# Sliding-window attention gated by a GLU: q weights ahead of x tile 3, four more products of zeros, and reciprocals and one tile's transposes moved from the DMA queue to the matrix engine

## The chip, the cores and the metric

The kernel runs on one core of a Trainium2 chip. A core has a matrix engine (PE, TensorE; its weight loads are listed as PEld), a vector engine (DVE), a scalar engine (ACT), a general engine (POOL), and a queue engine (SP) that issues all of this kernel's DMAs. The engines run side by side, each through its own instructions in order, and wait for each other by semaphores. The metric is the device time in microseconds (us).

## The reference

The inputs are bf16: x (2048 x 512), wqkv (512 x 1536), wo (512 x 512), the GLU's w_gate and w_up (512 x 1792) and w_down (1792 x 512).

```python
xn  = layernorm(x)
# attention: 32 heads of 16, each position looks at 8 keys, 2 apart, behind it
qkv = xn @ wqkv
logits[s, w] = q[s] . k[s - 2*w] * 16**-0.5          # -1e9 where s - 2*w < 0
attn = softmax(logits over w)
o[s] = sum_w attn[s, w] * v[s - 2*w]
s   = o @ wo
# GLU, on the same xn
g   = silu((gelu(xn @ w_gate) * (xn @ w_up)) @ w_down)
out = x + s * g
```

Attention and GLU share the layer-normed xn; the residual is x itself.

## The kernel before

The 2048 rows are 16 tiles of 128 rows, in four chunks j of 512 rows. Each chunk goes through three stages: `glu` (14 columns of 128 features: eight 512-column products into g_ps and u_ps, Gelu and a copy on ACT, their product h on DVE), `qkv` (12 groups of four products; of the *next* chunk) and `down` (four tiles; the down products over h, silu on ACT, the product with wo, the gate and the residual on DVE, the store). Everything else (layer norm, transposes, logits, softmax, the weighted sums over v) is hung between these steps by a table, `side`: `at((stage, j, i), function, ...)` puts a function ahead of step i of a stage, in the order of the calls, and `run` issues it there. The order of every engine's instructions is that of the program text; nothing is reordered.

**Transposes.** The products need xn transposed (xnT). `transpose` (L204) does it on PE, four 128-column products with the identity into one accumulator tile, then a copy to SBUF on ACT or DVE (L217, L219). `transpose_by_dma` (L229) does it with four transposing DMAs on SP's queue. Chunk 0, and tiles 4 to 6 of chunk 1, go by PE; tile 7, the last of chunk 1, and chunks 2 and 3 go by DMA.

**Softmax division.** `denominators` (L313) sums the exponentials on PE, and DVE takes the reciprocals (L328), 128 x 128 values rs. They must be spread over four row groups and 512 columns (rb) before `divide` (L379) multiplies them into the weighted sums o_ps on DVE. `spread_reciprocals` (L331) spreads them by four 128-column products on PE (sp_ps) and a copy on ACT (L339); the last chunk does it so. `spread_by_dma` (L342) stores rs to DRAM (L344) and loads it back four times (L347); chunks 0 to 2 do it so. Chunk 0's division stands ahead of the 11th qkv group of chunk 1, those of chunks 1 and 2 ahead of the 7th qkv group of the next chunk, that of chunk 3 ahead of its last GLU column.

**Accumulators.** The tiles of the pool `mm` (g_ps, u_ps, qkv_ps, y_ps, s_ps, tr, den_ps, sp_ps, warm_ps) are four buffers in turn: a new one waits until what was in its buffer four tiles earlier has been read.

**The head.** SP requests x tiles 0 to 3 one by one (L95), then wqkv in three parts (q, k, v; L97), then the rest of x and the GLU weights. PE meanwhile multiplies zeros (`warm_up`, L221; 17 products of 256 columns, later twice four of 128). DVE takes the moments of a tile (L177), ACT the square root (L179), DVE normalizes (L199), PE transposes. The q products of the first two tiles (q_ps) follow, then tiles 2 and 3:

Of the kernel before, what the change touches and what calls it, by code (L numbers as in the profile page):

```python
# [10 lines left out]
BF16 = mybir.dt.bfloat16  # L11
F32 = mybir.dt.float32

P = 128
H = 32
# [3 lines left out]
WL = 4  # L19
WH = 2  # L20
PAD = 16
TQ = 512
# [6 lines left out]
def kernel(  # L29
# [13 lines left out]
    nc = tc.nc  # L43
    B, S, D = A_x.shape
    DF = B_w_gate.shape[1]
    NT, NC, NF, NJ = S // P, D // P, DF // P, S // TQ
    TPQ = TQ // P
# [5 lines left out]
    def pool(name, bufs, **kw):  # L53
        return ctx.enter_context(tc.tile_pool(name=name, bufs=bufs, **kw))
# [10 lines left out]
    op = pool("op", 1)  # L65
# [3 lines left out]
    dram = pool("dram", 1, space=bass.MemoryType.DRAM)  # L69
# [5 lines left out]
    wqkv_sb = wts.tile([P, NC, 3 * D], BF16, name="wqkv_sb")  # L75
# [2 lines left out]
    wd_sb = wts.tile([P, NF, D], BF16, name="wd_sb")  # L78
    wo_sb = wts.tile([P, NC, D], BF16, name="wo_sb")
    vT = dram.tile([D, SV], BF16, name="vT")  # L80
    rs_d = [dram.tile([P, P], BF16, name=f"rs_d{j}") for j in range(NJ - 1)]

    def load_x(t, n=1):
        nc.sync.dma_start(
            out=x_sb[:, t : t + n, :],
            in_=x2d[t * P : (t + n) * P, :].rearrange("(t p) d -> p t d", p=P),
        )

    def load_w(dst, src, lo, hi):
        nc.sync.dma_start(  # L90
            out=dst[:, :, lo:hi], in_=src.rearrange("(k p) n -> p k n", p=P)[:, :, lo:hi]
        )

    for t in range(TPQ):
        load_x(t)  # L95
    for i in range(3):
        load_w(wqkv_sb, A_wqkv, i * D, (i + 1) * D)  # L97
    load_x(TPQ, TPQ)
    for i, (lo, hi) in enumerate(((0, DF // 2), (DF // 2, DF))):
# [4 lines left out]
    def load_late_weights():  # L104
        nc.sync.dma_start(out=wd_sb[:], in_=B_w_down.rearrange("(k p) n -> p k n", p=P))
        for g in range(NC):
            nc.sync.dma_start(
                out=wo_sb[:, g, :],
                in_=bass.AP(
                    tensor=A_wo.tensor, offset=g * 4 * D, ap=[[D, 4], [DH * D, H], [1, D]]  # L110
                ),
            )
# [7 lines left out]
        out=vT.rearrange("(k p) n -> p k n", p=P)[:, :, 0:PAD],  # L120
        in_=warm[:, 0 : NC * PAD].rearrange("p (k n) -> p k n", k=NC),
# [54 lines left out]
    def first_moments(t):  # L176
        nc.vector.bn_stats(out=stats[:, t, :], in_=x_sb[:, t, :])  # L177
        nc.vector.bn_aggr(out=mv[:, t, :], in_=stats[:, t, :])
        nc.scalar.activation(  # L179
            out=std[:, t, :], in_=mv[:, t, 1:2], func=AF.Sqrt, bias=epsc[:], scale=1.0  # L180
        )
# [39 lines left out]
    def warm_up(n, cols):  # L221

        ps = mm.tile([P, TQ], F32, name="warm_ps", tag="mm")
        for _ in range(n):
            nc.tensor.matmul(
                ps[:, 0:cols], lhsT=warm[:, 0:P], rhs=warm[:, 0:cols], start=True, stop=True
            )
# [22 lines left out]
    st = [dict(pk={}, pv={}) for _ in range(NJ)]  # L250

    def qkv(j, fo, i0=0, n=TQ, ps=None):
        which, c = divmod(fo, NC)
        if fo == 0 and i0 == 0:
            st[j]["q"] = qp.tile([P, NC, TQ], BF16, name="q_sb")
        if ps is None:
            ps = mm.tile([P, n], F32, name="qkv_ps", tag="mm")[:]
            project(ps, wqkv_sb, fo * P, j, i0, n)
        if which == 0:
            nc.scalar.activation(out=st[j]["q"][:, c, i0 : i0 + n], in_=ps, func=AF.Copy)  # L260
        elif which == 1:
            lo = PAD + j * TQ + i0
            nc.scalar.activation(out=k_sb[:, c, lo : lo + n], in_=ps, func=AF.Copy)  # L263
        else:
            vst = sm4.tile([P, TQ], BF16, name="vst")
            nc.scalar.activation(out=vst[:], in_=ps, func=AF.Copy)  # L266
            lo = PAD + j * TQ
            nc.sync.dma_start(out=vT[c * P : (c + 1) * P, lo : lo + TQ], in_=vst[:])

    def load_v(j, wls=range(WL)):  # L270

        if wls[0] == 0:
            st[j]["va"] = vap.tile([P, DH, VW], BF16, name="v_arr")
        va = st[j]["va"]
        for wl in wls:
            nc.sync.dma_start(
                out=va[H * wl : H * (wl + 1), :, :],
                in_=bass.AP(
                    tensor=vT.tensor,
                    offset=PAD + j * TQ - WL * DIL - DIL * wl,  # L280
                    ap=[[SV * DH, H], [SV, DH], [1, VW]],
                ),
            )
# [55 lines left out]
        nc.scalar.activation(out=rb[:], in_=sp[:], func=AF.Copy)  # L339
        st[j]["rb"] = rb  # L340

    def spread_by_dma(j):  # L342

        nc.sync.dma_start(out=rs_d[j][:, :], in_=st[j]["rs"][:])  # L344
        rb = op.tile([P, TQ], BF16, name="rbd")
        for i in range(WL):
            nc.sync.dma_start(  # L347
                out=rb[H * i : H * (i + 1), :].rearrange("h (q i) -> h q i", q=4),
                in_=rs_d[j].rearrange("(q h) i -> h q i", h=H),
            )  # L350
        st[j]["rb"] = rb

    def av_product(j, g, wh):
        pv = prod.tile([P, 4, TQ], BF16, name="pv", tag="prod")
        lo = WL * DIL * (1 - wh)
        nc.vector.tensor_tensor(  # L356
            out=pv[:],
            in0=st[j]["E"][:, wh, :].unsqueeze(1).to_broadcast([P, 4, TQ]),
            in1=st[j]["va"][:, 4 * g : 4 * g + 4, lo : lo + TQ],
            op=ALU.mult,  # L360
        )
        st[j]["pv"][g, wh] = pv
# [73 lines left out]
    def at(key, fn, *args):  # L436
        side.setdefault(key, []).append((fn, args))
# [5 lines left out]
    for i in range(TPQ):  # L443
        at(("qkv", 0, i), normalize, TPQ + i)
        at(("glu", 0, 7 + i), moments, 2 * TPQ + i)
        if i < TPQ - 1:
            at(("glu", 0, i), transpose, TPQ + i)
        at(("glu", 0, 8 + i), normalize, 2 * TPQ + i)
        at(("glu", 1, 0), transpose_by_dma, 2 * TPQ + i)
        at(("glu", 1, 10 + i), moments, 3 * TPQ + i)  # L450
        at(("qkv", 2, 2 * i), normalize, 3 * TPQ + i)
        at(("glu", 2, 0), transpose_by_dma, 3 * TPQ + i)
# [4 lines left out]
    for i in range(8):  # L457
        at(("glu", 0, 12 + i) if i < 2 else ("qkv", 1, (0, 1, 3, 4, 5, 6)[i - 2]),
           av_product, 0, i // 2, i % 2)
    at(("qkv", 1, 3), denominators, 0)  # L460
    at(("qkv", 1, 3), spread_by_dma, 0)
    at(("qkv", 1, 10), av_sums, 0)
    at(("qkv", 1, 10), divide, 0)

    for j in range(1, NJ):
        for w in range(W):
            early = j > 1 and w < 3
            at(("qkv", j, 9 + w) if early else ("down", j - 1, w // 3), qk_product, j, w)
        for i in range(TPQ):
            at(("down", j - 1, i), load_v, j, [i])  # L470
        at(("glu", j, 0), logits, j)
        for i in range(8):
            at(("glu", j, 2 + i), av_product, j, i // 2, i % 2)
        at(("glu", j, 11), denominators, j)
        at(("glu", j, 11), av_sums, j)
        if j + 1 < NJ:
            at(("glu", j, 11), spread_by_dma, j)
            at(("qkv", j + 1, 6), divide, j)
        else:
            at(("glu", j, 12), spread_reciprocals, j)  # L480
            at(("glu", j, 13), divide, j)


    HT = TPQ // 2
    HQ = HT * P
    warm_up(17, TQ // 2)
    first_moments(0)
    first_moments(1)
    first_normalize(0)
# [27 lines left out]
    for i in range(NC):  # L517
        run("qkv", 0, i)
        run("qkv", 0, NC + i)
        qkv(0, 2 * NC + i)  # L520
    at(("glu", 0, 0), transpose_by_dma, 2 * TPQ - 1)
    at(("glu", 0, 0), load_v, 0)
    at(("glu", 0, 0), load_late_weights)
    for j in range(NJ):
        for fc in range(NF):
            run("glu", j, fc)
# [36 lines left out]
```

## Time and profile before

| | us |
|---|---|
| median of three runs (230.1 to 230.49) | 230.17 |
| the profiled execution | 230.49 |
| its span, first to last instruction | 228.8 |
| PE busy | 222.7 (97% of the span) |
| DVE busy | 147.6 (65%) |
| ACT busy | 130.6 (57%) |
| POOL busy | 21.7 (10%) |

Busy time is the time in which an engine has an instruction of its own at work. In a row of a timeline the first number is the start after the beginning of the span, the second how long the row's instructions took from the first start to the last end, and `x4` how many they are; in brackets, where it is there, how long the engine stood idle before them and who ended that. Products on PE are pipelined: the next starts before the last has ended, so what a group costs PE is read from its start to the next group's start. `SPq` rows are DMA requests, not transfers. A few per cent of the products' records are missing from a trace, so that a group may show three products where it has four.

### The profile page before, as it was taken

How to read it: one execution, taken by the hardware profiler on the slowest of the kernel's cores; microseconds unless marked ns; L12 is line 12 of the kernel's file. 1: busy time of each engine (PE TensorE's matmuls, PEld its weight loads, DVE VectorE, ACT ScalarE, POOL GpSimd, SP SyncE). 2: the span in 40 equal slices, each digit the busy share in tenths (PEclk: the TensorE clock that was granted, in tenths of full speed). 3: DMA queues.
4: the chain of work that ended last, by engine and by line, in shares of the span. 5: the costliest groups of instructions: out<-in, count | busy, mean ns of one | idle time of the engine just before them, and what ended most of it. 6: DMA issues, size and time to landing. Idle time of an engine off the chain costs nothing.

```text
span 228.8 us, 3516 instructions
## 1 busy us (share of the span) xinstructions
PE 222.7 (97%) x1303; PEld 106.8 (47%) x1323; DVE 147.6 (65%) x234; ACT 130.6 (57%) x215; POOL 21.7 (10%) x61
## 2 busy tenths in 40 slices
PE   7999999999999999999999999999999999999994
PEld 5865444444444444444444444444444444444453
DVE  4593996894898198865678169735449429845232
ACT  3679779764514867476721687646741387647211
POOL 1048944100000000110000000000000000000000
PEclk9999999999999999999999999999999999999999
DMA  6999599922366611110266711110038910000001
GB/s 157 357 375 376 140 175 199 315 98 80 91 153 152 135 23 29 27 29 0 92 162 152 162 29 23 26 34 6 30 104 193 202 30 3 0 0 4 23 23 46
DMA packets 29857, 24.33 MB, mean 106 GB/s; under 512 B 9488, under 2 KB 29840, under 8 KB 29840
## 3 DMA queue, kind: packets, MB, share of 16 engines
q1 hardware_dynamic: 29840, 24.11, 41.0%
q8 instruction: 10, 0.16, 0.3%
q14 instruction: 7, 0.06, 0.1%
HBM read 18.61 MB, written 4.31 MB: 100 GB/s over the span
## 4 chain that ended last, share of the span: by engine, by line
PE 94%; ACT 2%; DVE 1%; DMA 1%; issue 1%; ACTq 0%; DVEq 0%
PE y_ps L411 21%; PE u_ps L242 21%; PE g_ps L242 20%; PE qkv_ps L242 17%; PE s_ps L421 6%; PE L_ps L299 3%; PE o_ps L370 3%; DMA x_sb<-in_A_x_dram 1%; PE q_ps L242 1%; PE tr L208 1%; DVE stats L177 1%; ACT L395 1%; ACT u L397 1%; PE den_ps L319 0%; ACT xnT L217 0%
## 5 line engine op out<-in xcount | busy, mean ns | idle before, releaser
L242 PE MATMUL u_ps<-xnT,wu_sb 128*128 128x512 bf16 x223 | 57.3, 379 | 0.2
L242 PE MATMUL g_ps<-xnT,wg_sb 128*128 128x512 bf16 x214 | 56.5, 379 | 0.6 <-issue 0.2
L411 PE MATMUL y_ps<-wd_sb,h 128*128 128x512 bf16 (+1 forms) x234 | 50.9, 366 | 0.2
L399 DVE TENSOR_TENSOR h<-ge,u 128x512 bf16<-128x512 bf16 x56 | 23.8, 424 | 37.5 <-ACT u L397 36.8
L288 DVE TENSOR_TENSOR pk<-q_sb,k_sb 128x2048 bf16<-128x2048 bf16 x32 | 37.8, 1221 | 7.0 <-ACT k_sb L263 7.0
L395 ACT ACTIVATE ge<-g_ps 128x512 bf16<-128x512 f32 x56 | 33.6, 600 | 14.7 <-PE g_ps L242 14.0
L397 ACT ACTIVATE u<-u_ps 128x512 bf16<-128x512 f32 x56 | 33.6, 599 | 14.6 <-PE u_ps L242 14.4
L242 PE MATMUL qkv_ps<-xnT,wqkv_sb 128*128 128x512 bf16 (+1 forms) x203 | 40.5, 354 | 0.2
L356 DVE TENSOR_TENSOR pv<-E,v_arr 128x2048 bf16<-128x2048 bf16 x32 | 38.6, 1217 | 0.0
L411 PEld LDWEIGHTS <-h 128*128 128x128 bf16 x238 | 23.3, 98 | 25.3
L418 ACT ACTIVATE sl<-y_ps 128x512 bf16<-128x512 f32 (+1 forms) x17 | 9.7, 573 | 44.0 <-PE y_ps L411 44.0
L242 PEld LDWEIGHTS <-wu_sb 128*128 128x128 bf16 x224 | 21.9, 98 | 26.6 <-issue 0.3
L242 PEld LDWEIGHTS <-wg_sb 128*128 128x128 bf16 x224 | 21.2, 98 | 26.8 <-issue 3.0
L242 PEld LDWEIGHTS <-wqkv_sb 128*128 128x128 bf16 x224 | 21.7, 98 | 19.6 <-issue 0.4
L429 DVE TENSOR_TENSOR m<-s_ps,sl 128x512 bf16<-128x512 f32 (+1 forms) x17 | 11.2, 658 | 22.4 <-PE s_ps L421 22.4
L421 PE MATMUL s_ps<-wo_sb,oT 128*128 128x512 bf16 (+1 forms) x68 | 16.6, 366 | 0.0
L193 POOL TENSOR_TENSOR rstd<-rstd,mhalf 128x1 f32<-128x1 f32 x12 | 7.7, 638 | 78.9 <-DVE rstd L190 76.7
L266 ACT ACTIVATE vst<-qkv_ps 128x512 bf16<-128x512 f32 x16 | 9.6, 598 | 6.4 <-PE qkv_ps L242 6.4
L263 ACT ACTIVATE k_sb<-qkv_ps 128x512 bf16<-128x512 f32 (+1 forms) x20 | 10.2, 517 | 3.4 <-PE qkv_ps L242 3.2
L260 ACT ACTIVATE q_sb<-qkv_ps 128x512 bf16<-128x512 f32 (+1 forms) x16 | 8.7, 545 | 3.5 <-PE qkv_ps L242 3.3
L421 PEld LDWEIGHTS <-oT 128*128 128x128 bf16 x68 | 6.6, 98 | 7.2
L382 DVE TENSOR_TENSOR oT<-o_ps,rbd 128x1024 bf16<-128x1024 f32 x6 | 7.1, 1219 | 3.7 <-PE qkv_ps L242 3.7
(52 smaller groups left out, 119.3 us busy)
## 6 DMA issues: line engine op xcount, KB each, us to landing
v_arr<-vT SPq DMA_DIRECT2D x16, 520.0 KB, 5.1
vT<-vst SPq DMA_DIRECT2D x16, 128.0 KB, 2.8
out_dram<-o_t SPq DMA_DIRECT2D x15, 128.0 KB, 2.3
wg_sb<-in_B_w_gate_dram SPq DMA_DIRECT2D x2, 896.0 KB, 10.8
wu_sb<-in_B_w_up_dram SPq DMA_DIRECT2D x2, 896.0 KB, 10.9
wd_sb<-in_B_w_down_dram SPq DMA_DIRECT2D x1, 1792.0 KB, 16.9
wqkv_sb<-in_A_wqkv_dram SPq DMA_DIRECT2D x3, 512.0 KB
x_sb<-in_A_x_dram SPq DMA_DIRECT2D x3, 512.0 KB, 11.6
```

What stands on the lines that cost most here:

```text
L242: nc.tensor.matmul(ps, lhsT=w[:, dk, lo : lo + P], rhs=xnT[j][:, dk, i0 : i0 + n], start=(dk == 0), stop=(dk == NC - 1),)
L263: nc.scalar.activation(out=k_sb[:, c, lo : lo + n], in_=ps, func=AF.Copy)
L266: nc.scalar.activation(out=vst[:], in_=ps, func=AF.Copy)
L288: nc.vector.tensor_tensor(out=pk[:], in0=st[j]["q"][:], in1=k_sb[:, :, off : off + TQ], op=ALU.mult)
L356: nc.vector.tensor_tensor(out=pv[:], in0=st[j]["E"][:, wh, :].unsqueeze(1).to_broadcast([P, 4, TQ]), in1=st[j]["va"][:, 4 * g : 4 * g + 4, ...
L395: nc.scalar.activation(out=ge[:], in_=g_ps[:], func=AF.Gelu_apprx_tanh)
L397: nc.scalar.activation(out=u[:], in_=u_ps[:], func=AF.Copy)
L399: nc.vector.tensor_tensor(out=h[:], in0=ge[:], in1=u[:], op=ALU.mult)
L411: nc.tensor.matmul(y[:], lhsT=st[j][fc][:, tt * P : (tt + 1) * P], rhs=wd_sb[:, fc, cols], start=(fc == 0), stop=(fc == NF - 1),)
L418: nc.scalar.activation(out=sl[:, cols], in_=y[:], func=AF.Silu)
L421: nc.tensor.matmul(s[:], lhsT=st[j]["oT"][:, g, tt * P : (tt + 1) * P], rhs=wo_sb[:, g, cols], start=(g == 0), stop=(g == NC - 1),)
L429: nc.vector.tensor_tensor(out=m[:], in0=s[:], in1=sl[:, cols], op=ALU.mult)
```

## The change

The q part of wqkv is requested ahead of x tile 3. Four products of zeros of 128 columns are added behind the seventeen at the beginning. Tile 7 is transposed on PE, ahead of the fourth GLU column of chunk 0, not by DMA. In chunks 0 to 2 the reciprocals are spread by PE and ACT; chunk 0's spread stands ahead of the ninth qkv group of chunk 1 and its division where it was; in chunks 1 and 2 spread and division stand ahead of the 13th and 14th GLU column, as in chunk 3. The loads of chunk 0's v and of the late weights are issued ahead of the first GLU column without the table; the DMA transposes that stood ahead of them are gone.

```diff
-    rs_d = [dram.tile([P, P], BF16, name=f"rs_d{j}") for j in range(NJ - 1)]
...
-    for t in range(TPQ):
+    for t in range(TPQ - 1):
         load_x(t)
-    for i in range(3):
+    load_w(wqkv_sb, A_wqkv, 0, D)
+    load_x(TPQ - 1)
+    for i in range(1, 3):
         load_w(wqkv_sb, A_wqkv, i * D, (i + 1) * D)
...
-    def spread_by_dma(j):
-
-        nc.sync.dma_start(out=rs_d[j][:, :], in_=st[j]["rs"][:])
-        rb = op.tile([P, TQ], BF16, name="rbd")
-        for i in range(WL):
-            nc.sync.dma_start(
-                out=rb[H * i : H * (i + 1), :].rearrange("h (q i) -> h q i", q=4),
-                in_=rs_d[j].rearrange("(q h) i -> h q i", h=H),
-            )
-        st[j]["rb"] = rb
...
-        if i < TPQ - 1:
-            at(("glu", 0, i), transpose, TPQ + i)
+        at(("glu", 0, i), transpose, TPQ + i)
...
-    at(("qkv", 1, 3), spread_by_dma, 0)
+    at(("qkv", 1, 8), spread_reciprocals, 0)
...
-        if j + 1 < NJ:
-            at(("glu", j, 11), spread_by_dma, j)
-            at(("qkv", j + 1, 6), divide, j)
-        else:
-            at(("glu", j, 12), spread_reciprocals, j)
-            at(("glu", j, 13), divide, j)
+        at(("glu", j, 12), spread_reciprocals, j)
+        at(("glu", j, 13), divide, j)
...
     warm_up(17, TQ // 2)
+    warm_up(4, P)
     first_moments(0)
...
-    at(("glu", 0, 0), transpose_by_dma, 2 * TPQ - 1)
-    at(("glu", 0, 0), load_v, 0)
-    at(("glu", 0, 0), load_late_weights)
+    load_v(0)
+    load_late_weights()
     for j in range(NJ):
```

## The prediction

> **What bounds the kernel now.** I read the sums of busy time first, then the waits of the matrix engine (PE), then the chain that ended last, and last the timeline around each place that the change touches.
>
> From the page, busy time per engine and the chain's shares:
>
> ```profile
> PE 222.7 (97%) x1303; PEld 106.8 (47%) x1323; DVE 147.6 (65%) x234; ACT 130.6 (57%) x215; POOL 21.7 (10%) x61
> ...
> PE 94%; ACT 2%; DVE 1%; DMA 1%; issue 1%; ACTq 0%; DVEq 0%
> ```
>
> Everything that PE waited for in the whole run (line, whom it waited for, total us, times, longest):
>
> ```profile
> PE warm_ps L225 <- DVE k_sb L162: 1.1, 1, 1.1
> PE tr L208 <- DVE xn L199: 0.3, 1, 0.3
> PE g_ps L242 <- issue: 0.2, 1, 0.2
> ```
>
> The reader is to see that after the first transpose, 5.21 us in, all of PE's listed waits are 0.2 us. A busy PE need not be a PE at its peak, but in the timeline each group of four 512-column products takes 0.86 to 0.87 us start to start, without pause. So from 7 us on, what is added to PE's queue makes the program longer by its own duration, and what is taken off the other engines or the DMA queue gives nothing back. Only the head can gain.
>
> The head, PE's timeline (start, us, line, tile, count):
>
> ```profile
> 5.21 0.61 PE L208 MATMUL tr<-ident,xn 128*128 128x128 bf16 x4 [0.29 <-DVE xn L199]
> 5.62 0.63 PE L225 MATMUL warm_ps<-warm 128*128 128x128 bf16 x4
> 6.04 0.63 PE L208 MATMUL tr<-ident,xn 128*128 128x128 bf16 x4
> 6.47 0.58 PE L225 MATMUL warm_ps<-warm 128*128 128x128 bf16 x4
> 7.15 1.91 PE L242 MATMUL q_ps<-xnT,wqkv_sb 128*128 128x256 bf16 x16
> 8.89 0.39 PE L208 MATMUL tr<-ident,xn 128*128 128x128 bf16 x4
> ```
>
> The first chunk's q products start at 7.15. In the chain they follow "ACT xnT L217" at 6.71, the copy of the second tile's transposes, whose first half ends at 7.10. The clock can be read here too: four 128-column products start 0.42 us before the next group up to 6.47, and 0.22 us before it at 8.89 (the next group starts at 9.12). PE runs at half speed until about 7 us (the page's row of the granted clock shows full speed in every slice and doesn't resolve the head).
>
> **The parts that cost.** PE's price of a spread stands in the last chunk, which already does it on PE:
>
> ```profile
> 205.22 1.03 PE L242 MATMUL u_ps<-xnT,wu_sb 128*128 128x512 bf16 x4
> 206.08 0.39 PE L334 MATMUL sp_ps<-rs,spread 128*128 128x128 bf16 x4
> 206.31 1.03 PE L242 MATMUL g_ps<-xnT,wg_sb 128*128 128x512 bf16 x4
> ```
>
> A row's duration holds the drain of its last product; what PE loses is start to start, 206.31 - 206.08 = 0.23 us. Three more chunks: 3 x 0.23 = 0.69. Transposing the last tile of chunk 1 on PE is four products like those of its neighbour:
>
> ```profile
> 22.14 0.39 PE L208 MATMUL tr<-ident,xn 128*128 128x128 bf16 x4
> 22.36 1.03 PE L242 MATMUL g_ps<-xnT,wg_sb 128*128 128x512 bf16 x4
> ```
>
> 22.36 - 22.14 = 0.22. Together 0.69 + 0.22 = 0.91 us, all on the path. The Trainium skill, "TensorE: Matmul & The Clock Gate", section "Back-to-back issue gap", gives about 81 ns for each 128-column product in a stream with weight loads; by that the sixteen would cost an estimated 1.30 us. The two rows, at 56 to 57 ns, are of these very instructions, and decide.
>
> **The new waits on PE.** Each spread waits for DVE's reciprocal, and all of PE's later work is queued behind it. The reciprocals:
>
> ```profile
> 49.94 0.95 DVE L328 RECIPROCAL rs<-den_ps 128x128 bf16<-128x128 f32 x1
> ...
> 96.39 0.95 DVE L328 RECIPROCAL rs<-den_ps 128x128 bf16<-128x128 f32 x1
> ```
>
> Chunk 0: done at 50.89; its spread stands before the ninth qkv group, which is five groups of 0.86 after the one at 47.94, about 52.26: 1.4 us to spare. Chunk 1: done at 97.34, and the spread takes the place of the g products at 97.93: 0.6 to spare, the smallest margin. Chunk 2: done at 150.40, slot at 152.01: 1.6. DVE's order up to the reciprocal doesn't change, so I take 0. Without that margin each us late would be a us lost.
>
> **The added ACT work.** Four copies, 0.59 (the last chunk's rb row) and 0.60 us (xnT). The three rb copies fall where ACT idles 0.2 to 0.3 us before each eviction; in the last chunk the same copy took up two such gaps and PE did not wait. The xnT copy falls into a crowded place: ACT runs without idling from 18.73 to 24.89 and then has 0.27, 0.33 and 0.21 of idle ahead of its next three. It pushes the next Gelu from 25.15 by at most 0.6 - 0.27 = 0.33 us. PE has four accumulator tiles in turn, so a copy may be two products of 0.86 late before PE feels it: 0, with 0.33 as the end.
>
> **The divisions.** Two DVE instructions of 1.22 us in each chunk, whichever rb they read (1219 ns with the DMA's, 1217 with PE's). For chunk 0 they can start when o_ps is done, near 56, not at 57.89. For chunks 1 and 2 they go ahead of the last h product and delay it by 2.35; h is first read by the down products, 10 us later (111.74 and 165.82). Nothing for PE.
>
> **What leaves the DMA queue.** Three rs_d stores, twelve rbd loads, four DMA transposes: SP is held from 21.57 to 27.66 by the transposes, and after 50.92, 97.36 and 150.43 by the others. Behind them stand the v loads of chunk 0 (issued from 27.83, read by DVE at 43.59), the late weights (read from 57.67) and the v stores of chunk 1. All could go earlier; none has a waiter on PE. Moving the v and weight loads ahead of the loop leaves their place in SP's queue behind the v stores. 0.
>
> **The head.** Four more products of zeros at half speed: 4 x 0.107 = 0.43 us. The seventeen start at 1.12 and take 0.213 each, so PE could issue the next at 4.74; 4.74 + 0.43 = 5.17, and the first transpose starts at 5.21 on xn, done at 5.16. They fit into the idle piece: 0, at most 0.43 should x come earlier.
>
> The q weights move ahead of x tile 3. PE loaded them at 6.92 without waiting, and the products were released by ACT at 7.10; at most 0.05 to gain. Tile 3 pays: by the rates of the stretches, 0.63 MB had moved by 5.0 us, and from there 370 to 385 GB/s; the four x tiles and the q weights together are 1.05 MB, moved by about 6.1 in either order. A tile alone is 2.1 us from issue to landing (the x row of the chain), 0.3 to 0.5 of it after its data; I estimate tile 3 in place at 6.5, where DVE turned to it at 6.41:
>
> ```profile
> 6.41 0.66 DVE L177 BATCH_NORM_STATS2 stats<-x_sb 128x6 f32<-128x512 bf16 x1
> ...
> 7.59 0.16 DVE L184 RECIPROCAL rstd<-std 128x1 f32<-128x1 f32 x1 [0.29 <-ACT std L179]
> 7.79 0.41 DVE L199 TENSOR_SCALAR xn<-x_sb,mv,rstd 128x512 bf16<-128x512 bf16 x1
> ```
>
> Behind it DVE idles 0.29, and the third tile's xn, done at 8.20, is taken by PE at 8.89: 0.69 more. So tile 3 may come about 0.9 late, near 7.3, at no cost. As late end I take the landing of a further 0.5 MB at 370 GB/s: 6.5 + 1.4 = 7.9, 0.5 us lost. I take 0.
>
> **Sum.** +0.91 us. The profiled execution took 230.49 us (span 228.8 and 1.69 around it), the highest of three whose median is 230.17; it should become 231.40, and the median 231.08. The three runs spread by 0.39 us, and a change under 0.2%, 0.46 us, can't be told from none.
>
> **Rivals.**
> *The clock opens earlier* (the one that ends on the other side, not slower). The extra products close PE's idle piece before 5.21. If full speed came by then, the first two sets of transposes would take half; PE would take up the second tile's at about 5.74 (its xn is ready at 5.68), ACT would have copied half of it by about 6.55, and the q products would start near 6.6: 0.55 gained, 230.53, within 0.2%. It decides from 0.45 us on. For it: PE is idle just there. Against it: full speed came less than 2 us after that idle piece in the run shown, after 3.8 us of products that hadn't brought it, so the piece doesn't seem to have restarted a count.
> The Trainium skill, same page, section "What's actually happening", has a free-running window of 3413 ns that must be busy and is not reset by the program's start. By that the filling would gain 0 where the window's edge lies as it did here, and the late opening agrees; no view here shows the window.
>
> *Tile 3 comes too late.* Its data queue behind the q weights and PE waits for the third transpose: 0.91 + 0.5, 231.58. For it: half a MB goes ahead of it. Against it: 0.9 us of slack.
>
> *ACT holds PE at the start of the GLU.* The fourth xnT copy comes where ACT has no idle time: 0.91 + 0.33, 231.41. Against it: the accumulator tiles in turn.
>
> *The DMA traffic mattered.* Faster needs over 1.37 us won elsewhere, and PE's waits after the head are 0.2 us in all.
>
> **How the numbers follow.** The forecast holds with 0.70 (own range 230.9 to 231.3, from the spread of the runs); the clock 0.13, of which 0.10 within 0.2%; tile 3 late 0.09; ACT 0.05; faster through something unseen 0.03. Slower: 0.70 + 0.03 + 0.09 + 0.05 = 0.87; same 0.10; faster 0.03. The range goes from the clock's 230.5 to tile 3's 231.6.
>
> **What the changed profile would show.** Four rows of L334's kind with four products each and 0.23 to the next start; a fourth set of transposes ahead of the fourth GLU column; PE's waits still under 2 us in all, with none on rs or sp; first transpose still near 5.2 and q products near 7.15; a span near 229.7. Wrong if the q products start before 6.8, if PE waits before 8.89 on the third tile, or if a spread waits for its reciprocal.

## The result and the profile after

The changed kernel takes 231.30 us (median; 231.03 to 231.56), the kernel before, timed beside it, 230.26 us: ratio 1.0043, 95% interval 1.003 to 1.0056. The prediction's 231.08 against 230.17 was a ratio of 1.0040. The profiled execution took 231.30 us with a span of 229.6 (229.59 in the trace, against 228.78 before).

From the page of the changed kernel, busy time per engine and the chain's shares:

```profile
PE 223.6 (97%) x1322; PEld 107.8 (47%) x1343; DVE 147.5 (64%) x234; ACT 132.5 (58%) x219; POOL 22.2 (10%) x61
...
PE 95%; ACT 2%; issue 1%; DVE 0%; ACTq 0%; DVEq 0%
```

All that PE waited for, as the trace lists it:

```profile
PE warm_ps L226 <- DVE k_sb L163: 1.1, 1, 1.1
PE q_ps L243 <- ACT xnT L218: 0.3, 1, 0.3
```

No wait on a reciprocal, a spread or an added copy has appeared (the 0.3 us on ACT's copy are those of the head): the program is still PE's own work from end to end, and PE has more of it. Here are the spreads of chunks 0, 1 and 2 in PE's timeline:

```profile
52.23 0.39 PE L335 MATMUL sp_ps<-rs,spread 128*128 128x128 bf16 x4
52.45 1.89 PE L243 MATMUL qkv_ps<-xnT,wqkv_sb 128*128 128x512 bf16 x8
...
98.12 0.39 PE L335 MATMUL sp_ps<-rs,spread 128*128 128x128 bf16 x4
98.34 1.03 PE L243 MATMUL g_ps<-xnT,wg_sb 128*128 128x512 bf16 x4
...
152.42 0.39 PE L335 MATMUL sp_ps<-rs,spread 128*128 128x128 bf16 x4
152.64 1.03 PE L243 MATMUL g_ps<-xnT,wg_sb 128*128 128x512 bf16 x4
```

and tile 7's transposes with what stands behind them:

```profile
23.83 0.39 PE L209 MATMUL tr<-ident,xn 128*128 128x128 bf16 x4
24.05 1.03 PE L243 MATMUL g_ps<-xnT,wg_sb 128*128 128x512 bf16 x4
```

Each costs PE 0.22 us, start to start. A ruler that leaves the head and the end out is the stretch from the start of the first q product to the start of the last down product (y_ps): from 7.15 to 224.80 us before, 217.65 us; from 6.89 to 225.43 after, 218.54 us. The difference, 0.89 us, is sixteen products of 0.056 us and nothing else.

The head is not as before:

```profile
5.29 0.61 PE L209 MATMUL tr<-ident,xn 128*128 128x128 bf16 x4
5.69 0.50 PE L226 MATMUL warm_ps<-warm 128*128 128x128 bf16 x4
6.03 0.39 PE L209 MATMUL tr<-ident,xn 128*128 128x128 bf16 x4
6.25 0.39 PE L226 MATMUL warm_ps<-warm 128*128 128x128 bf16 x4
6.89 1.91 PE L243 MATMUL q_ps<-xnT,wqkv_sb 128*128 128x256 bf16 x16 [0.25 <-ACT xnT L218]
```

The zeros filled PE's idle piece as reckoned, and the first transposes start 0.08 later because the first x tile landed that much later, at 3.01 instead of 2.93. But the second set of transposes already runs at full speed, and the q products start 0.26 us sooner than in the profile before.

The sum of the two profiles: +0.89 on PE, -0.26 at the head, and the span grew by 0.81. So 0.18 us more must lie behind PE's last down product, which no step of the prediction has. It lies behind the last store. SP's rows for the last four stores, before and then after:

```profile
218.98 7.75 SPq L431 DMA_DIRECT2D out_dram<-o_t  x4
```

```profile
219.61 7.75 SPq L421 DMA_DIRECT2D out_dram<-o_t  x4
```

The requests end at 226.73 and 227.36, 0.63 apart (0.89 - 0.26); the spans end at 228.78 and 229.59, 0.81 apart. From the last store's start to the end of the program it is 2.39 us before and 2.57 after. At its end SP checks the semaphores of its DMAs one by one. The trace has eight in turn, and each check takes 0.06 us. Before, the last store's semaphore was the last to be checked; after, with nineteen DMAs fewer, three more are checked behind it, 3 x 0.062 = 0.19 us. The store itself takes as long as before, 1.54 us from its start to its landing (227.93 and 228.56); after the landing its own check starts at 228.58 and the three others at 228.64, 228.70 and 228.76.

Two questions are left: what the head's edits are worth, since a single profile can't tell, and whether the place of the last store really sets the end.

### The profile page after: what moved, and what is told of

The parts are those of the page before. It is cut to its first block, busy times and chain, and to the rows that moved or that the text cites. A ratio compares the mean times of both kernels' runs of the same rounds, so it can differ in the third digit from the quotient of the medians.

```text
span 229.6 us, 3534 instructions
## 1 busy us (share of the span) xinstructions
PE 223.6 (97%) x1322; PEld 107.8 (47%) x1343; DVE 147.5 (64%) x234; ACT 132.5 (58%) x219; POOL 22.2 (10%) x61
## 4 chain that ended last, share of the span: by engine, by line
PE 95%; ACT 2%; issue 1%; DVE 0%; ACTq 0%; DVEq 0%
PE y_ps L401 21%; PE u_ps L243 21%; PE g_ps L243 19%; PE qkv_ps L243 17%; PE s_ps L411 6%; PE L_ps L300 3%; PE o_ps L360 3%; PE warm_ps L226 2%; PE q_ps L243 1%; ACT u L387 1%; PE tr L209 1%; ACT xnT L218 1%; ACT L385 1%; PE den_ps L320 0%; PE sp_ps L335 0%
## 5 line engine op out<-in xcount | busy, mean ns | idle before, releaser
L372 DVE TENSOR_TENSOR oT<-o_ps,rb 128x1024 bf16<-128x1024 f32 x8 | 9.4, 1217 | 2.1 <-PE o_ps L360 2.1
```

## The experiments

**Theories.** By the first, the change costs 0.89 us on PE and 0.18 at the end, and gains at the head what the earlier landing of the q weights gives; the clock opens where it falls in each execution. By its rivals, the zeros make the clock open sooner; a wait on ACT, DVE or the DMA queue takes part in the cost; the longer end was chance.

### The spreads alone

```diff
-            at(("glu", j, 11), spread_by_dma, j)
-            at(("qkv", j + 1, 6), divide, j)
+        at(("glu", j, 12), spread_reciprocals, j)
+        at(("glu", j, 13), divide, j)
...
-    at(("qkv", 1, 3), spread_by_dma, 0)
+    at(("qkv", 1, 8), spread_reciprocals, 0)
```

> The kernel before with the reciprocals of chunks 0 to 2 spread by PE alone. If only PE's own time counts: 3 x 0.22 = 0.67 us more on PE, so 230.9 (ratio 1.0029), every spread followed by the next product after 0.23 us and PE waiting for no reciprocal. If a spread waits for its reciprocal: more than 0.75 on PE, with a wait on rs or sp in PE's list. If the twelve loads and three stores taken off the DMA queue are worth something: under 0.6 on PE. A second theory speaks of the end of the program: fifteen DMAs fewer move the last store to another of the queue's eight semaphores, and each semaphore checked after its landing takes 0.06 us; by it the time from the last store's issue to the end grows by up to 0.4 us.

Measured: 231.41 us against 230.50, ratio 1.0043 (1.003 to 1.0055). PE's stretch is 218.33, 0.68 more than before, as twelve products of 0.056 make it; from the last store to the end it is 2.54. That is 0.84 of the 0.91. The profiled execution was the slowest of the five, 231.83, and the new thing is at its head:

```profile
6.47 0.61 PE L224 MATMUL warm_ps<-warm 128*128 128x128 bf16 x4
7.65 1.92 PE L241 MATMUL q_ps<-xnT,wqkv_sb 128*128 128x256 bf16 x16 [0.57 <-DMA wqkv_sb<-in_A_wqkv_dram]
```

With the head unchanged, the q products waited here for the q weights, to 7.65. ACT's copy was there at 7.10 as in the profile of before. So the landing of the q weights, which never showed in that profile, is a bound in some executions.

### Tile 7 alone

```diff
-        if i < TPQ - 1:
-            at(("glu", 0, i), transpose, TPQ + i)
+        at(("glu", 0, i), transpose, TPQ + i)
...
-    at(("glu", 0, 0), transpose_by_dma, 2 * TPQ - 1)
-    at(("glu", 0, 0), load_v, 0)
-    at(("glu", 0, 0), load_late_weights)
+    load_v(0)
+    load_late_weights()
```

> The kernel before with tile 7 of chunk 1 transposed on PE alone (and the v and late weight loads issued ahead of the loop). If only PE's own time counts: 0.22 us more on PE. If ACT holds PE at the start of the GLU: up to 0.33 more than that, to be seen between the fourth transpose and the tenth GLU column. By the theory of the end, four DMAs fewer put the last store four semaphores earlier: 4 x 0.06 = 0.25 us more from its issue to the end of the program, together 0.47 us, 230.7 (ratio 1.0020); without it 230.5 (1.0010).

Measured: 231.37 us against 230.50, ratio 1.0035 (1.0021 to 1.0048). In the trace PE's stretch is 217.94, 0.29 more: 0.22 for the transposes, 0.06 a short wait in the third chunk's GLU. From the last store to the end it is 2.64, the 0.25 more that four semaphores make. No wait of PE followed the transposes at 23.89. That is 0.54 us of the 0.87; the profiled execution was the fastest of the five, and the other 0.3 us is not settled by its trace. The clock opened at 3.9 us here, without any added zeros; and still the q products waited for their weights, until 6.94.

### The zeros alone

```diff
     warm_up(17, TQ // 2)
+    warm_up(4, P)
     first_moments(0)
```

> The kernel before with four more products of zeros alone. If they fit into PE's idle piece and do nothing to the clock: the same time within 0.1%, and a clock that opens anywhere between 5 and 7 us, as it falls in each execution. If they make the clock open sooner: the q products start at 6.9 or earlier, in this profile and in every other with the added products, and the median falls by 0.2 to 0.3 us (ratio 0.9990).

Measured: 230.47 us against 230.50, ratio 1.0007 (0.9995 to 1.0019). The zeros alone change nothing that can be measured. The q products of its profile waited for the weights again:

```profile
6.93 1.92 PE L242 MATMUL q_ps<-xnT,wqkv_sb 128*128 128x256 bf16 x16 [0.31 <-DMA wqkv_sb<-in_A_wqkv_dram]
```

### The order of requests alone

```diff
-    for t in range(TPQ):
+    for t in range(TPQ - 1):
         load_x(t)
-    for i in range(3):
+    load_w(wqkv_sb, A_wqkv, 0, D)
+    load_x(TPQ - 1)
+    for i in range(1, 3):
         load_w(wqkv_sb, A_wqkv, i * D, (i + 1) * D)
```

> The kernel before with the q weights requested ahead of x tile 3 alone. Both theories expect the q products to start when ACT has copied the first half of the second tile's transposes, not sooner, and tile 3's moments about 0.5 us later, at 6.9 to 7.0, with no wait of PE for the third transpose (slack 0.9 us): the same time within 0.1%. If PE does wait, the third set of transposes comes later than 1.74 us behind the first q product. The clock opens at about 6.9 as before if it depends on the filling, and anywhere between 5 and 7 if it does not.

Measured: 230.14 us against 230.50, ratio 0.9982 (0.9963 to 1.0001). DVE's rows for tile 3, and PE's for the q products and the third set of transposes:

```profile
7.16 0.69 DVE L179 BATCH_NORM_STATS2 stats<-x_sb 128x6 f32<-128x512 bf16 x1 [0.67 <-DMA x_sb<-in_A_x_dram]
...
8.67 0.41 DVE L201 TENSOR_SCALAR xn<-x_sb,mv,rstd 128x512 bf16<-128x512 bf16 x1
```

```profile
6.80 1.92 PE L244 MATMUL q_ps<-xnT,wqkv_sb 128*128 128x256 bf16 x16 [0.40 <-DMA wqkv_sb<-in_A_wqkv_dram]
8.62 0.40 PE L210 MATMUL tr<-ident,xn 128*128 128x128 bf16 x4
```

Tile 3's moments are 0.75 us later than before, and PE felt only 0.07 of it (8.62 is 1.82 behind the first q product, not 1.74). This edit was expected to be worth nothing; it seemed to be worth something, and was tried again:

> The order of requests alone once more, for the size of its gain: 0.1 to 0.3 us under before (ratio 0.9985 to 0.9995), the q products starting at 6.9 or earlier.

Measured: 230.04 us against 230.40, ratio 0.9979 (0.9962 to 0.9996), the q products at 6.58. Both put its gain at 0.36 us (the first interval just reaches none, the second doesn't); the next experiment has 0.2.

### Both edits of the head

The two diffs above together.

> The kernel before with both edits of the head (order and zeros) and none of the others. If the clock opens where it falls and the q weights' landing is what the new order moves: the q products start between 6.7 and 7.1, the closing stretch after the last store is the 2.38 us of before, and the time is 0.1 to 0.4 us under before (ratio 0.998 to 0.9995), like the order alone. If the zeros do something of their own: at least 0.2 us below the order alone.

Measured: 230.23 us against 230.41, ratio 0.999 (0.9973 to 1.0007). With the zeros it is no better than the order alone.

### The changed kernel without the head's edits

The two diffs above undone in the changed kernel.

> The changed kernel with both edits of the head undone: spreads and tile 7 on PE, the old order of requests, seventeen products of zeros. By the sum 16 x 0.056 = 0.89 us on PE from the first q product to the last down product (218.54 against 217.65), plus three more semaphores after the last landing, 0.18 (2.57 against 2.39 us from the last store to the end): 1.07 us over before, ratio 1.0047. If the head's edits gain nothing, it equals the changed kernel; if they gain 0.2 to 0.3, it is that much slower than it.

Measured: 231.52 us against 230.41, a difference of 1.11; ratio 1.0043 (1.0026 to 1.006). PE's stretch is 218.56, the end 2.57: both as expected, 1.09 us in all by the trace. The changed kernel's 231.30, 0.2 below it, is from another set of runs; the next kernel, from the same set and with the head's edits, is 0.32 below it, of which the shorter end is 0.19, so 0.13 is left for the head's edits there. Alone the two parts cost 0.91 and 0.87, together only 1.11: the ends don't add up (three checks and four alone, three together), and the 0.3 us that tile 7's trace left open isn't found in the whole kernel.

### Three loads more

```diff
+    spare = const.tile([P, 3, 8], BF16, name="spare")
+
+    def spare_load(i):
+        nc.sync.dma_start(out=spare[:, i, :], in_=x2d[0:P, 0:8])
...
+    for i in range(3):
+        at(("glu", 2, 8 + i), spare_load, i)
```

> The changed kernel with three loads of 2 KB more, put in the third chunk's GLU, which nothing reads (work added, none left out). If the position of the last store among the eight semaphores sets the closing stretch: it goes back from 2.57 to 2.38 us, and PE's stretch stays 218.54: 0.19 us less, ratio to before 1.0035 where the changed kernel has 1.0043. If the longer close of the changed kernel was chance or has to do with something else: 2.57 stays.

Measured: 231.20 us, ratio 1.0028 (1.001 to 1.0045). From the last store to the end it is 2.38 us, as in every kernel whose last store has the last semaphore (2.39, 2.37, 2.38, 2.38, 2.37, 2.38, 2.37, 2.38), while it is 2.57, 2.57, 2.54 and 2.64 in the four where it has another. Adding three useless loads made the end 0.19 us shorter. PE's stretch is 218.64, not 218.54; 0.07 of the 0.10 is a wait for tile 3, whose transposes start at 8.72, 1.82 behind the first q product. The median fell by 0.1 us, which the intervals don't separate from none; that the place of the last store sets the end is read from the traces.

### The q weights in halves

```diff
+    def load_wk(k, n, lo, hi):
+        nc.sync.dma_start(
+            out=wqkv_sb[:, k : k + n, lo:hi],
+            in_=A_wqkv.rearrange("(k p) n -> p k n", p=P)[:, k : k + n, lo:hi],
+        )
...
+    load_wk(0, 2, 0, D)
+    load_x(TPQ - 1)
+    load_wk(2, 2, 0, D)
...
-        load_x((2 + i) * TPQ, TPQ)
+        if i == 1:
+            load_x(2 * TPQ, 2 * TPQ)
```

> The kernel before with the q weights requested in two halves of 256 KB, the first ahead of x tile 3 and the second behind it, and the last two requests for x in one, so that the number of DMAs and with it the close stay the same. If the landing of the q weights is what holds the q products: the first half is there by about 6.2, and the products start with ACT's copy, at 6.6 to 7.15 by when the clock opens, never released by the weights; 0.2 to 0.5 us under before (ratio 0.998 to 0.999). If the landing is not the bound: the same as before within 0.1%. The clock opens anywhere between 4 and 7 us here too, if the zeros have no part in it.

Measured: 230.64 us against 230.41, ratio 1.0013 (0.9989 to 1.0037). The mechanism came out, the time did not:

```profile
PE qkv_ps L252 <- DMA wqkv_sb<-in_A_wqkv_dram: 1.2, 1, 1.2
...
PE q_ps L252 <- ACT xnT L227: 0.2, 1, 0.2
```

The q products were released by ACT, at 6.60, the earliest that any profile but one has; the first half of the weights had landed at 5.1. But the k weights, one request further back, now landed only at 9.86 us, and PE waited 1.2 us for them. A bound moved up by one request put the next one in its place. The twelve executions spread from 230.21 to 232.31, the profiled one took 231.29; how many of them waited like this, one trace can't tell.

### Less on PE instead of more

The order of requests, the last chunk's spread by DMA too, and tile 6 by DMA too, with tile 7's transposes behind the v loads:

```diff
-        if i < TPQ - 1:
+        if i < TPQ - 2:
             at(("glu", 0, i), transpose, TPQ + i)
...
+        at(("glu", j, 11), spread_by_dma, j)
+        at(("qkv", j + 1, 6) if j + 1 < NJ else ("glu", j, 13), divide, j)
...
-    at(("glu", 0, 0), transpose_by_dma, 2 * TPQ - 1)
+    at(("glu", 0, 0), transpose_by_dma, 2 * TPQ - 2)
     at(("glu", 0, 0), load_v, 0)
+    at(("glu", 0, 0), transpose_by_dma, 2 * TPQ - 1)
```

> The opposite of the change's tail: the kernel before with the new order of requests, with the last chunk's reciprocals too spread by DMA and tile 6 too transposed by DMA (tile 7's transposes behind the v loads), and two requests for x in one, so that eight DMAs more leave the last store on the same semaphore. If only PE's own time counts: eight products fewer, 0.45 us less from the first q product to the last down product (217.20), the close 2.38, and with 0.2 from the order 229.7 to 229.9 (ratio 0.997). If the DMAs matter: PE waits for rb in the last chunk's product with wo, or for the transposes of tile 6 or 7 at the next chunk's q products, or for the v loads, and the gain is lost or turned.

Measured: 230.31 us against 230.40, ratio 0.9993 (0.9984 to 1.0002). PE's stretch is 217.77, not 217.20. 0.49 of the missing 0.57 us stands at one place, the sums o_ps of chunk 0 (the other 0.08 at the head, around the third set of transposes):

```profile
53.50 1.70 PE L373 MATMUL o_ps<-pv,hsum 128*32 128x512 bf16 x28
55.50 0.40 PE L373 MATMUL o_ps<-pv,hsum 128*32 128x512 bf16 x4 [0.31 <-DVE pv L359]
```

and its cause 11 us earlier, on DVE:

```profile
44.15 0.41 DVE L202 TENSOR_SCALAR xn<-x_sb,mv,rstd 128x512 bf16<-128x512 bf16 x1 [2.57 <-DMA xnT<-xn]
44.48 0.42 DVE L402 TENSOR_TENSOR h<-ge,u 128x512 bf16<-128x512 bf16 x1
44.81 1.22 DVE L359 TENSOR_TENSOR pv<-E,v_arr 128x2048 bf16<-128x2048 bf16 x1
```

Tile 7's transposes, requested behind the v loads at 30.7 us, landed at 43.2 to 44.0. Until then its xn buffer was not free for tile 11, DVE stood 2.57 us behind that, and its eight pv products started at 44.81, not at 43.59. A DMA that nobody on PE waits for cost PE half a microsecond through a buffer.

### Less on PE, where the DMA has room

The order of requests and the last chunk's spread by DMA, tile 6 left alone:

```diff
-    rs_d = [dram.tile([P, P], BF16, name=f"rs_d{j}") for j in range(NJ - 1)]
+    rs_d = [dram.tile([P, P], BF16, name=f"rs_d{j}") for j in range(NJ)]
...
+        at(("glu", j, 11), spread_by_dma, j)
+        at(("qkv", j + 1, 6) if j + 1 < NJ else ("glu", j, 13), divide, j)
...
+    for i in range(3):
+        at(("glu", 2, 8 + i), spare_load, i)
```

> The kernel before with the new order of requests and the last chunk's reciprocals too spread by DMA; three loads of 2 KB that nothing reads are added in the third chunk, so that eight DMAs more leave the last store on the same semaphore. If only PE's own time counts: four products fewer, 0.22 us less from the first q product to the last down product (217.43 against 217.65), close 2.38, and with 0.2 to 0.35 from the order 229.9 (ratio 0.9975, under the 0.998 of the order alone). If the division of the last chunk comes too late: a wait of PE in the first s_ps of the last chunk, and no gain over the order alone.

Measured: 229.76 us against 230.48, ratio 0.9967 (0.9953 to 0.9981), faster than both kernels. PE's stretch is 217.43, the end 2.38. The division of the last chunk waits 0.29 us for the loads, and nobody waits for it:

```profile
208.89 2.35 DVE L389 TENSOR_TENSOR oT<-o_ps,rbd 128x1024 bf16<-128x1024 f32 x2 [0.29 <-DMA rbd<-rs_d]
211.17 0.42 DVE L406 TENSOR_TENSOR h<-ge,u 128x512 bf16<-128x512 bf16 x1
```

### The heads side by side

When the q weights landed, when the clock opened (the start of the full-speed entry in the trace's record of the granted clock, which the slices of the page don't resolve), when the q products started, and what released them; times in us:

| kernel | zeros added | q weights | weights land | clock opens | q products | released by |
|---|---|---|---|---|---|---|
| before | no | behind tile 3 | 6.88 | 6.86 | 7.15 | ACT's copy |
| spreads alone | no | behind tile 3 | 7.60 | 6.92 | 7.65 | q weights |
| tile 7 alone | no | behind tile 3 | 6.89 | 3.90 | 6.94 | q weights |
| without the head's edits | no | behind tile 3 | 6.82 | 4.61 | 6.87 | q weights |
| zeros alone | yes | behind tile 3 | 6.89 | 5.97 | 6.93 | q weights |
| order alone | no | ahead | 6.76 | 5.52 | 6.80 | q weights |
| order again | no | ahead | 6.27 | 4.36 | 6.58 | ACT's copy |
| less on PE, with tile 6 | no | ahead | 6.67 | 5.23 | 6.71 | q weights |
| less on PE, last spread | no | ahead | 6.45 | 5.36 | 6.62 | ACT's copy |
| both edits of the head | yes | ahead | 6.47 | 6.07 | 6.90 | ACT's copy |
| changed | yes | ahead | 6.56 | 5.92 | 6.89 | ACT's copy |
| three loads more | yes | ahead | 6.86 | 4.61 | 6.90 | q weights |
| halves | no | first half ahead | 5.13 (first half) | 4.96 | 6.60 | ACT's copy |

In two of these kernels, without the head's edits and with three loads more, the row of the products names ACT:

```profile
6.87 1.92 PE L241 MATMUL q_ps<-xnT,wqkv_sb 128*128 128x256 bf16 x16 [0.49 <-ACT xnT L216]
...
6.90 1.92 PE L248 MATMUL q_ps<-xnT,wqkv_sb 128*128 128x256 bf16 x16 [0.69 <-ACT std L180]
```

But the half of ACT's copy that the products need was done at 6.58 and 6.42, and they don't read std. PE's first load of q weights started at 6.86 and 6.90, 0.04 us after their landing and 4 ns ahead of the products, and that load's wait is put down to the DMA. So the weights were last here too: in four of the five profiles with the old order and in three of the seven with the new one.

With the old order the q products start at 7.11 on the mean of five, with the new one at 6.77 on the mean of seven (the halves left out): 0.34 us, the size of what the order alone gained in time. A single profile weighs much in this: without the 7.65 the difference is 0.20.

With the zeros the clock opened from 4.6 to 6.1, without them from 3.9 to 6.9. The same record shows how long it stayed open: 221.87 us in six of the thirteen profiles and 225.28 in seven, which is 65 and 66 times 3.413 us. From this I infer that it opens and closes at marks 3.413 us apart, which fall elsewhere in the program in each execution. Where it opened at 6.86 and 6.92, the marks before were at 3.45 and 3.51, 2.33 and 2.39 us after PE's first product, and it did not open there; where it opened soonest, at 3.90, PE had worked for 2.78 us. The added zeros are issued from 4.7 on, behind those marks, so they couldn't have made the two late openings earlier; and without them the clock opened at 5.36 and 5.52, right behind PE's idle piece. By this reckoning the zeros have no part in the openings seen here.

## Why the prediction was right, and where it was not

**"The parts that cost": right.** 0.91 us were reckoned, 0.89 measured on PE, product by product, and the spreads and tile 7 alone showed their shares, 0.68 and 0.22. The price in the neighbouring rows held: sixteen products at 0.056 us, not at the 81 ns that the Trainium skill's "Back-to-back issue gap" ("TensorE: Matmul & The Clock Gate") gives.

**"The new waits on PE", "The added ACT work", "The divisions": right.** In the changed kernel the reciprocal of chunk 1 was done at 97.52 and its spread started at 98.12, the 0.6 us of margin that was reckoned. ACT took tile 7's copy at 24.52 and the next Gelu at 25.11, and PE did not wait. Chunk 0's division started at 56.30, 1.6 sooner, for nobody's benefit.

**"What leaves the DMA queue": 0 was wrong.** No engine waited for these DMAs, but the end of the program did: 0.18 us, by the place of the last store among the semaphores that SP checks one by one. The step looked for waiters among the engines and left out the close of the program.

**"The head", the q weights: "at most 0.05 to gain" was wrong.** It was read from one profile, in which the clock opened late and ACT's copy was last. Even there the load at 6.92 was not "without waiting": it started 0.04 us after the landing at 6.88, and the landing was only 0.22 ahead of ACT's copy at 7.10. In the three old-order profiles where the clock opened earlier the weights were last, and with the spreads alone they were last by 0.5 us (7.65 against 7.15) although the clock opened late. The order was worth 0.13 to 0.36 us.

**"The head", tile 3: no cost was right to 0.07 us, the slack was mis-sized.** DVE got to tile 3 at 6.97 in the changed kernel and at 7.16 with the order alone, not at 6.5. The slack of 0.9 was measured from q products at 7.15; they now start 0.3 sooner, PE is at the third set of transposes that much sooner, and the slack shrinks with it: with tile 3 at 7.16 PE waited 0.07 us. The late tile and the early products have one cause: tile 3 landed 0.36 to 0.39 us behind the q weights in each of the seven profiles with the new order, so where the weights release the products, the slack is gone.

**"The head", the zeros, and the rival of the clock.** The zeros fitted as reckoned and changed no time. The q products of the changed kernel did start 0.26 sooner and the clock did open sooner than in the profile before, as the rival has it. But it opened sooner in seven kernels without the zeros too, and the marks leave the zeros no part in it. The prediction saw no view of a window; the lengths for which the clock stayed open, 65 and 66 times 3.413 us, are one. The Trainium skill, "TensorE: Matmul & The Clock Gate", section "What's actually happening", has a window of 3413 ns that runs free of the program's start; the opening times, from 3.9 to 6.9 us with PE's first product at 1.12 in each, spread over 3.0 us, a little under one such window. The same section has the transition vary by ±500 ns; here it varied by three times that.

**The sum.** 0.91 came out as 0.89 + 0.18 less 0.13 to 0.36, between 0.7 and 0.95 us; in time the changed kernel was 1.04 slower in one set of runs and, with the end shortened by 0.19, 0.79 in another. The size was met in part because the two terms left out have opposite signs. The direction rests on the part that was shown piece by piece.

## What to carry to other kernels

Where one engine is busy from end to end, price a step by the start-to-start time of the same instruction on that engine; moving work onto it costs that price, and moving work off it gains it only if the queue that takes the work lands it before a buffer is wanted again. What is read from one profile about a race between a transfer and an engine is one draw: before a landing is called free, ask by how much the other side of the race varies. And count the DMAs: the end of the program checks their semaphores in a fixed order, and the place of the last store can cost as much as four products.

## What the runs showed of the hardware

PE's clock opened between 3.9 and 6.9 us after the start of the span in thirteen profiles whose first product started at 1.12. It stayed open for 221.87 or 225.28 us, 65 or 66 times 3.413. The request of 512 KB for the q weights, issued at 2.65 us in the old order, landed at 6.82, 6.88, 6.89, 6.89 and 7.60, and released the products 0.04 to 0.05 us later in four of these five. SP's check of one semaphore at the end took 0.06 us, and the last store landed 1.54 us after its start, in the changed kernel as before.
